# Banded attention feeding a two-layer MLP in split float32: slices of d_ff taken two at a time

## The chip, the cores and the metric

The kernel runs on one core of one Trainium2 chip. The metric is the device time of one execution in microseconds (us). The core has five engines that work side by side: TensorE (PE, matmuls; its weight loads are listed as PEld), VectorE (DVE), ScalarE (ACT), GpSimd (POOL) and SyncE (SP, which issues nearly all DMAs). Each engine works through its own queue in the order in which the built program lists its instructions.

## The reference

Attention over 4 batches, 8 heads, 768 positions and head dimension 64, with a distance bias and a mask (8 global keys and the 96 last ones), then an MLP over the 3072 tokens. Cut to what matters:

```
scores = q @ k.T / sqrt(D) - slope[h] * dist;  scores = where(keep, scores, -1e9)
a = softmax(scores);  x = a @ v                        # (3072, 512)
h = x @ w_in                                           # (3072, 2048), the first layer
g = h * clip(h + 3, 0, 6) / 6                          # the gate
out = g @ w_out                                        # (3072, 512), the second layer
```

The MLP's weights and activations are float32. The kernel gets float32 accuracy from the faster rounded format fp32r by splitting each operand into a high and a low part (`w1h` and `w1l`, `xh` and `xl`, `gh` and `gl`) and adding three products.

## The kernel before, in words

The tokens are cut into eight blocks of 384 (`blocks`, numbered 0 to 7). Each block takes the 16 slices of d_ff (`f`, 128 wide) in turn. For one slice of one block:

- `first(f, x)` (line 167) issues 12 matmuls of 384 columns into one of two PSUM banks, the tile `hp`.
- `gate` (178, 179) turns `hp` into `g`: ACT adds 3 and clips below, DVE clips above and multiplies. There is one buffer for `g`, so the next gate begins after the last reader of this one.
- `high` (185 on POOL, 187 on ACT while weights are being decoded) makes `gh`, and `rest` (192, DVE) makes `gl`.
- `second(f, acc, gh, gl)` (line 199) issues 9 matmuls of 512 columns that add the slice to three accumulators.

Below, F*n* is the first layer of slice *n* and S*n* its second one. `halves` writes them in the order F0, F1, S0, F2, S1, F3, S2 and so on: each second layer stands one first layer behind its own.

The weights arrive as raw 64-bit words. `decode` (lines 395 to 428) makes 32 chunks of 512 columns from them: chunk 2*f* is the first-layer weight of slice *f*, chunk 2*f*+1 the second-layer one. A chunk costs five DVE instructions (409, 410, 418, 422, and 415, which writes the low part `w1l` or `w2l`) and three on ACT (375, 387, and 426, which writes the high part `w1h` or `w2h`). The methods `work` and `decoded_to` slip decode steps in between the layers as the code is written. The order of PE, SP and POOL is then fixed as written (`in_order`); DVE and ACT are put in an order by the scheduler while the program is built. What stands in a queue is not moved at run time.

Attention work is handed out in numbered units that run at the `yield`s of the layer loops: `scores` (842, PE, with DVE 853 and ACT 857 behind it), `split` (813 on POOL, 816 and 819 on DVE), `normalize` (877, POOL), `spread` (902 on DVE, then a DMA to `there`), `fetch` (a DMA back into `weights`) and `values` (929, PE).

The stages are: attention for the first nine head pairs with three slices of block 0 (to about 64 us); then the rest of block 0 and half of block 1, mixed by the string `ORDER`, while the weights are decoded (to about 157 us); then the rest of block 1 with attention for block 2 ("one", to about 198 us); then blocks 2 to 7 ("layers"), each with the attention of the block after it.

Of the kernel before, what the change touches and what calls it, by code (L numbers as in the profile page):

```python
# [25 lines left out]
NF = DF // P  # L26
# [33 lines left out]
class Kernel:  # L60
# [45 lines left out]
    def common(self, xs, banks):  # L106
        self.xp = self.pool("xp", xs)
        self.w1h, self.w1l, self.w2h, self.w2l = [], [], [], []
        self.gp = self.pool("gp", 3)
        self.gp1 = self.pool("gp1", 1)  # L110
        self.ps_h = self.pool("ps_h", banks, PSUM)

# [174 lines left out]
    def load(self, n, values):  # L287

        if n < len(self.blocks) * NPAIR:
            end = KW + (TB if n < EARLY else QW)  # L290
            for columns in (slice(KW + QW, LOAD),) if values else (slice(0, KW), slice(KW, end)) if n == 0 else (slice(0, end),):
                self.nc.sync.dma_start(out=self.place(n)[:, columns], in_=self.pairs[n, :, columns])
# [155 lines left out]
    def halves(self, steps, pool=False):  # L448


        for block, f, x, acc in steps:
# [11 lines left out]
                yield  # L463
            self.last = (block, f, acc, gh, gl)

    def end(self, steps):

        x, acc = steps[0][2:]
        late = []
        for k, (_, f, _, _) in enumerate(steps):  # L470
            g = self.gate(self.first(f, x), f == NF - 1)
            gh = self.high(g, True)
            late.append((f, acc, gh, self.rest(g, gh)))
            if k == 0:
                self.finish()
            elif k == 1:
                self.second(*late[0], (0, 1))
        self.second(*late[0], (2,))
        self.second(*late[1], (0, 1))
        self.second(*late[2], (0, 1))  # L480
        self.second(*late[1], (2,))
        self.second(*late[2], (2,))
# [11 lines left out]
    def banded(self, flag):  # L494

        self.banded_setup()
        start = len(self.nc.cur_bb.bb.instructions)
        self.common(2, 2)
        self.ps_s = self.pool("ps_s", 1, PSUM)
        self.ps_t = self.pool("ps_t", 1, PSUM)  # L500
        self.ps_x = self.pool("ps_x", 1, PSUM)
        self.turn, self.stage = {}, "attention"
        self.wake()
        self.raw, self.z, self.e, self.given, self.decoded = {}, {}, {}, [0.0, 0.0], 0
        self.last, self.op = None, None
        self.weights()
        with ExitStack() as early, ExitStack() as words:
            x0 = self.x_tiles(self.pool("x0", 1, ctx=early, side="right"))
            xs = [x0, self.x_tiles(), self.x_tiles()]
            self.decoding(words, 3, 2, side="right")  # L510
            self.decoding_steps = self.decode()

            self.decoded_all = words.close
            self.fetch(0)
            self.given[1] = LEAD
            self.allowed = 4 * NF + 3
            acc = []
            with ExitStack() as ctx:
                self.room += self.rooms(self.pool("more", 1, ctx=ctx), MORE - ROOMS, ROOMS)
                self.load(2, False)  # L520
                self.fetch(1)
                for n in range(ROOMS):
                    self.load(n, True)
                self.plain_distances(ctx)
                self.attending(ctx, 0, 9, 5)
                pairs = [Pair(self, n, xs[n // NPAIR], True) for n in range(EARLY)]
                todo = self.halves([(0, f, xs[0], acc) for f in range(FIRST)])

                def half():
                    if self.stage == "both":  # L530
                        next(todo, None)

                for n in range(-2, EARLY + 1):
                    if n + 2 < NPAIR:
                        self.distances(n + 2)
                    if n + 2 == EARLY:
                        self.stage = "both"
                        acc.extend(self.acc_tiles())
                    if n + 2 < EARLY:
                        weigh = []  # L540
                        for t in range(NT):
                            weigh.append(pairs[n + 2].scores(t))
                            if n == 0 and t < NT - 1:
                                self.spin(2)
                        if n < 0:
                            self.spin(5)
                        self.load_next(n + 2, False)
                        self.work(1.440, 0)
                    for t in range(NT):
                        if n + 2 < EARLY:  # L550
                            weigh[t]()
                            self.work(0, 0.64)
                            if t == NT - 1 and n == -2:
                                self.load(2, True)
                        if 0 <= n < EARLY:
                            pairs[n].turn(t)
                            if n == 0 and t < NT - 1:
                                self.spin(3)
                            self.work(0.396, 0)
                        if n + 1 in (0, 1):  # L560
                            pairs[n + 1].sum_up(t)
                            pairs[n + 1].normalize(t)
                        if t == 0:
                            if 2 <= n + 1 < EARLY:
                                pairs[n + 1].sum_up()
                            half()
                        if t == 1:
                            if n > 0:
                                pairs[n - 1].values()
                                self.work(1.350, 0.47)  # L570
                            if 2 <= n + 1 < EARLY:
                                for u in range(NT):
                                    pairs[n + 1].normalize(u)
                        if t == 2:
                            half()
                for _ in todo:
                    pass
            self.weights()
            self.allowed = 4 * (2 * NF + 1)
            acc1 = [pool.tile([P, BANK], F32, name=name) for pool, name in ((self.ps_s, "sp"), (self.ps_t, "tp"), (self.ps_x, "xp"))]  # L580
            self.given[1] = max(self.given)
            next_f, todo = [FIRST, 0], []
            for block in map(int, ORDER):
                todo.append((block, next_f[block], xs[block], (acc, acc1)[block]))
                next_f[block] += 1
            for _ in self.halves(todo):
                pass
            self.decoded_to(2 * NF - 1)
        self.attending(self.ctx, 2, 3, 2, side="right")
        self.bp = self.pool("bp", 3, side="right")  # L590
        self.there = self.pool("there", 2, bass.MemoryType.DRAM)
        self.op = self.pool("op", 3, side="right")
        self.stage = "one"
        units, pairs = self.rest_of_third(xs[2], NF - next_f[1])
        for k, _ in enumerate(self.halves([(1, f, xs[1], acc1) for f in range(next_f[1], NF)], True)):
            for unit in units[k]:
                unit()
        self.finish()
        pairs[-2].values("s")
        self.stage = "layers"  # L600
        x, ahead = xs[2], pairs[-1]
        for i in range(2, len(self.blocks)):
            units, x_next = [], None
            if i + 1 < len(self.blocks):
                x_next = self.x_tiles()
                units, ahead = self.attention(i + 1, x_next, ahead)
            else:
                units = [[]] * 4 + [[lambda: self.doubt(flag)]]
            acc = self.acc_tiles()
            steps = [(i, f, x, acc) for f in range(NF)]  # L610
            for k, _ in enumerate(self.halves(steps if x_next else steps[:-3], True)):
                for unit in units[k] if k < len(units) else ():
                    unit()
            if not x_next:
                self.end(steps[-3:])
            x = x_next
        self.in_order(start)
        return acc
# [390 lines left out]
```

## Time and profile before

| | |
|---|---|
| Median of three timed runs | 663.02 us (662.13 to 663.42) |
| Span of the profiled execution | 660.9 us, 11414 instructions |
| What lies between that span and the median | 2.1 us |
| PE busy | 649.6 us, 98% |
| DVE, ACT, POOL busy | 65%, 44%, 31% |
| Granted TensorE clock, mean | 0.998 |

The profiled execution has no time of its own beside its span, so a forecast for the span is carried to the median by adding those 2.1 us. Matmuls overlap in the pipeline, and the profile models their ends; "busy" on PE therefore says only that one was under way. A timeline row gives a start, a duration, the engine, the line and the operands. In the chain of work that ended last, each row is a start, a length, and what filled it.

### The profile page before, as it was taken

What the parts mean: (1) busy time and instruction counts of PE and PEld (TensorE: products, weight loads), DVE (VectorE), ACT (ScalarE), POOL (GpSimd) and SP (SyncE); (2) the same over time, 40 slices, a digit from 0 to 9 for tenths busy, and PEclk for the clock granted to TensorE, in tenths of its full rate; (3) what the DMA queues carried; (4) which work ended last, traced back from release to release, by engine and by line L of the source; (5) the groups of instructions that cost most, each with busy time, mean ns of one, the idle gap of its engine ahead of it and who ended that gap; (6) DMA issues with size and microseconds to landing.
All of it is one profiled execution on the core that took longest, in us unless ns stands there. A gap on an engine that the chain in (4) does not pass through costs nothing.

```text
span 660.9 us, 11414 instructions
## 1 busy us (share of the span) xinstructions
PE 649.6 (98%) x3933; PEld 581.9 (88%) x3933; DVE 427.6 (65%) x1147; ACT 288.1 (44%) x752; POOL 202.2 (31%) x377
## 2 busy tenths in 40 slices
PE   9989999999999999999999999999999999999997
PEld 7768899998989999999989999899998999989995
DVE  6888999998856876367654777367663777422222
ACT  6896877776434343344314333143422443121111
POOL 5663000002533433034331553134340444312110
PEclk9999999999999999999999999999999999999999
DMA  8676445432582566536553557615654265510001
GB/s 284 178 233 215 132 157 159 132 124 89 158 224 95 156 175 172 143 100 162 153 153 96 135 137 185 180 51 143 165 138 128 95 160 131 133 49 1 1 1 53
DMA packets 67316, 88.86 MB, mean 134 GB/s; under 512 B 10288, under 2 KB 52016, under 8 KB 67248
## 3 DMA queue, kind: packets, MB, share of 16 engines
q1 hardware_dynamic: 66960, 87.77, 46.5%
q8 instruction: 33, 0.54, 0.3%
q14 instruction: 35, 0.29, 0.1%
q10 hardware_dynamic: 288, 0.26, 0.1%
HBM read 65.08 MB, written 22.94 MB: 133 GB/s over the span
## 4 chain that ended last, share of the span: by engine, by line
PE 86%; DVE 9%; ACT 2%; issue 2%; POOL 0%; POOLq 0%; DVEq 0%; ACTq 0%
PE hp L167 37%; PE acc L199 33%; PE xp L929 3%; PE sp L842 2%; PE tp L929 2%; PE tp L842 2%; PE sp L199 1%; ACT n L857 1%; DVE wz L422 1%; PE tp L199 1%; DVE wz L418 1%; PE xp L199 1%; DVE wz L410 1%; DVE g L179 1%; DVE gl L192 1%
## 5 line engine op out<-in xcount | busy, mean ns | idle before, releaser
L178 ACT ACTIVATE g<-hp,small 128x384 f32<-128x384 f32 x127 | 73.7, 580 | 253.3 <-PE hp L167 227.0
L167 PE MATMUL hp<-xh,w1h 128*128 128x384 f32 x512 | 174.1, 340 | 0.4 <-ACT w1h L426 0.4
L167 PE MATMUL hp<-xh,w1l 128*128 128x384 f32 x512 | 173.0, 338 | 0.5 <-DVE w1l L415 0.5
L167 PE MATMUL hp<-xl,w1h 128*128 128x384 f32 x512 | 171.9, 336 | 0.0
L185 POOL TENSOR_SCALAR gh<-g 128x384 fp32r<-128x384 f32 x104 | 55.6, 535 | 311.2 <-DVE g L179 279.7
L199 PE MATMUL acc<-w2h,gl 128*128 128x512 f32 x336 | 133.2, 396 | 0.2 <-DVE gl L192 0.2
L199 PE MATMUL acc<-w2l,gh 128*128 128x512 f32 x336 | 132.4, 394 | 0.0
L199 PE MATMUL acc<-w2h,gh 128*128 128x512 f32 x336 | 131.9, 393 | 0.0
L179 DVE SCALAR_TENSOR_TENSOR g<-g,hp 128x384 f32<-128x384 f32 x128 | 69.8, 545 | 69.7 <-ACT g L178 69.1
L877 POOL TENSOR_SCALAR n<-n,sums 128x232 f32<-128x232 f32 (+1 forms) x186 | 99.4, 549 | 32.2 <-DVE sums L868 17.6
L192 DVE TENSOR_TENSOR gl<-g,gh 128x384 fp32r<-128x384 f32 x128 | 78.4, 613 | 47.5 <-POOL gh L185 47.5
L857 ACT ACTIVATE n<-n,least 128x232 f32<-128x232 f32 (+1 forms) x192 | 89.0, 465 | 41.6 <-DVE least L853 40.3
L167 PEld LDWEIGHTS hp<-xh,w1h 128*128 128x128 f32 x512 | 96.3, 188 | 6.4 <-issue 1.7
L167 PEld LDWEIGHTS hp<-xl,w1h 128*128 128x128 f32 x512 | 96.2, 188 | 3.8
L167 PEld LDWEIGHTS hp<-xh,w1l 128*128 128x128 f32 x512 | 96.0, 188 | 1.0 <-DVE w1l L415 0.8
L199 PEld LDWEIGHTS acc<-w2h,gl 128*128 128x128 f32 x336 | 63.0, 187 | 15.1 <-DVE gl L192 1.6
L199 PEld LDWEIGHTS acc<-w2h,gh 128*128 128x128 f32 x336 | 63.3, 188 | 10.5 <-POOL gh L185 0.3
L199 PEld LDWEIGHTS acc<-w2l,gh 128*128 128x128 f32 x336 | 63.2, 188 | 10.3
L902 DVE STREAM_TRANSPOSE blocks<-n 128x256 f32<-128x256 f32 x127 | 48.8, 422 | 27.0 <-POOL n L877 26.8
L813 POOL TENSOR_SCALAR kx<-load 64x504 fp32r<-64x504 f32 (+1 forms) x46 | 35.3, 767 | 100.3 <-PE hp L167 96.2
L853 DVE CUSTOM_DVE_ANT_0 n<-sp,d 128x232 f32<-128x232 f32 (+1 forms) x70 | 23.7, 376 | 36.7 <-PE sp L842 36.5
L857 ACT ACTIVATION_READ_ACCUMULATOR n<-n,least 128x1 f32 x192 | 36.1, 188 | 0.0
(118 smaller groups left out, 746.4 us busy)
## 6 DMA issues: line engine op xcount, KB each, us to landing
wst<-w SPq DMA_DIRECT2D x32, 512.0 KB, 3.5
there<-blocks SPq DMA_DIRECT2D x58, 256.0 KB, 2.6
load<-pairs SPq DMA_DIRECT2D x23, 636.0 KB, 5.1
load<-pairs SPq DMA_DIRECT2D x32, 384.0 KB, 4.3
weights<-there SPq DMA_DIRECT2D x48, 192.0 KB, 3.8
weights<-there SPq DMA_DIRECT2D x44, 160.0 KB, 3.2
out<-o SPq DMA_DIRECT2D x23, 256.0 KB, 2.2
load<-pairs SPq DMA_DIRECT2D x8, 444.0 KB, 4.4
```

What stands on the lines that cost most here:

```text
L167: self.nc.tensor.matmul(hp, lhsT=self.w1(w, f)[:, kt, :], rhs=a[:, kt, :], start=(n == 0), stop=(n == 3 * NKT - 1))
L178: nc.scalar.activation(out=g, in_=hp, func=AF.Relu, bias=self.three, scale=1.0)
L179: nc.vector.scalar_tensor_tensor(out=g, in0=g, scalar=6.0, in1=hp, op0=ALU.min, op1=ALU.mult)
L185: self.nc.gpsimd.tensor_scalar(out=gh, in0=g, scalar1=1.0, scalar2=0.0, op0=ALU.mult, op1=ALU.add)
L192: self.nc.vector.tensor_tensor(out=gl, in0=g, in1=gh.bitcast(F32), op=ALU.subtract)
L199: self.nc.tensor.matmul(acc[tt], lhsT=a[:, tk], rhs=self.w2(w, f), start=(f == 0 and j == 0), stop=(f == NF - 1 and j == 2))
L813: nc.gpsimd.tensor_scalar(out=part["kx"][own, c], in0=k[own, c], scalar1=1.0, scalar2=0.0, op0=ALU.mult, op1=ALU.add)
L842: nc.tensor.matmul(sp[j][:, lo:W], lhsT=q[:, t], rhs=part["kx"][:, c], start=(m == 0), stop=(m == 1))
L857: nc.scalar.activation(out=e[:, j, lo:W], in_=e[:, j, lo:W], func=AF.Exp, bias=self.least[:, i:i + 1], scale=-1.0, accum_out=self.sums[:, ...
L877: nc.gpsimd.tensor_scalar(out=e[:, j, lo:W], in0=e[:, j, lo:W], scalar1=over, scalar2=0.0, op0=ALU.mult, op1=ALU.add)
L902: nc.vector.transpose(out=blocks[:, :, s].rearrange("p b j q -> p j b q"), in_=e[:, :, c:c + P].rearrange("p j (b q) -> p j b q", b=4))
L929: nc.tensor.matmul(xps[j * D:(j + 1) * D, t * P:(t + 1) * P], lhsT=vt[0:K, t, j * D:(j + 1) * D], rhs=self.part(t, j, c, K), start=(c == 0 ...
```

## The change

`halves` is replaced by `twos` wherever it stood after the first nine pairs: in the mixed turns of blocks 0 and 1, in the rest of block 1, and in blocks 2 to 7. `twos` writes two first layers, each followed by its gate and both halves of `g`, then the two second layers of the pair before. To hold two pairs of results, the pool of `gh` and `gl` grows from three buffers each to four, and the pool of output tiles `o` shrinks from three to two. In `twos` the step that makes `gh` and `gl` stands right behind the gate in the code. There are four `yield`s for two slices, as before, but two of them follow both first layers and two follow both second ones.

```diff
-        self.gp = self.pool("gp", 3)
+        self.gp = self.pool("gp", 4)
...
+    def twos(self, steps, pool=False):
+        for i in range(0, len(steps), 2):
+            after = []
+            for block, f, x, acc in steps[i:i + 2]:
+                self.decoded_to(2 * f)
+                g = self.gate(self.first(f, x))
+                gh = self.high(g, pool)
+                after.append((block, f, acc, gh, self.rest(g, gh)))
+                self.work(2.1, 0.94)
+                if i == 0 and len(self.pending) == 1:
+                    self.last = self.pending[0]
+                    self.finish()
+                    self.pending = []
+            yield
+            yield
+            for self.last in self.pending:
+                self.finish()
+            self.pending = after
+            yield
+            yield
...
-            for _ in self.halves(todo):
+            self.pending = [self.last]
+            for _ in self.twos(todo):
...
-        self.op = self.pool("op", 3, side="right")
+        self.op = self.pool("op", 2, side="right")
...
-        for k, _ in enumerate(self.halves([(1, f, xs[1], acc1) for f in range(next_f[1], NF)], True)):
+        for k, _ in enumerate(self.twos([(1, f, xs[1], acc1) for f in range(next_f[1], NF)], True)):
...
-            for k, _ in enumerate(self.halves(steps if x_next else steps[:-3], True)):
+            for k, _ in enumerate(self.twos(steps if x_next else steps[:-3], True)):
```

Three places in the built program show it. The first is PE's queue in the mixed turns, where slice 7 of block 0 ends. Before (`hp_1383` is the result of slice 7, `hp_1430` that of slice 8; `gh_1364` and `gl_1366` belong to slice 3 of block 1):

```order
L167 MATMUL hp_1383<-xh_147,w1l0_141 128x384
L199 MATMUL sp_1027<-w2h0_142,gh_1364 128x512
L199 MATMUL sp_1027<-w2l0_143,gh_1364 128x512
L199 MATMUL sp_1027<-w2h0_142,gl_1366 128x512
L199 MATMUL tp_1028<-w2h0_142,gh_1364 128x512
L199 MATMUL tp_1028<-w2l0_143,gh_1364 128x512
L199 MATMUL tp_1028<-w2h0_142,gl_1366 128x512
L199 MATMUL xp_1029<-w2h0_142,gh_1364 128x512
L199 MATMUL xp_1029<-w2l0_143,gh_1364 128x512
L199 MATMUL xp_1029<-w2h0_142,gl_1366 128x512
L167 MATMUL hp_1430<-xh_147,w1h1_1023 128x384
```

Now, with `hp_1368` for slice 7 and `hp_1405` for slice 8:

```order
L167 MATMUL hp_1368<-xl_148,w1h0_140 128x384
L167 MATMUL hp_1368<-xh_147,w1l0_141 128x384
L167 MATMUL hp_1405<-xh_147,w1h1_1023 128x384
L167 MATMUL hp_1405<-xl_148,w1h1_1023 128x384
L167 MATMUL hp_1405<-xh_147,w1l1_1024 128x384
```

The nine matmuls of a second layer have gone from between the two first layers.

The second place is DVE's queue at the same point, where the low part of slice 8's first-layer weights is written (`w1l1_1024`; its raw words are in `wz_1359` before and `wz_1363` now). Before:

```order
L409 TENSOR_SCALAR wz_1400<-wz_1400 128x512
L192 TENSOR_TENSOR gl_1366<-g_1354,gh_1364 128x384
L410 TENSOR_SCALAR wz_1400<-wz_1400 128x512
L415 TENSOR_TENSOR w1l1_1024<-wz_1359,w1h1_1023 128x4x128
L418 SCALAR_TENSOR_TENSOR wz_1400<-wst_1336,wz_1400 128x512
L179 SCALAR_TENSOR_TENSOR g_1396<-g_1396,hp_1383 128x384
```

Now:

```order
L409 TENSOR_SCALAR wz_1395<-wz_1395 128x512
L179 SCALAR_TENSOR_TENSOR g_1381<-g_1381,hp_1368 128x384
L410 TENSOR_SCALAR wz_1395<-wz_1395 128x512
L415 TENSOR_TENSOR w1l1_1024<-wz_1363,w1h1_1023 128x4x128
L418 SCALAR_TENSOR_TENSOR wz_1395<-wst_1356,wz_1395 128x512
L192 TENSOR_TENSOR gl_1386<-g_1381,gh_1384 128x384
```

The gate of slice 7 stood behind slice 8's weights and now stands ahead of them. In the pair of slices 12 and 13 the queue reads the same way, with a line 418 between the gate and the weights.

The third place is POOL's queue in a block of the last stage, around the last head pair's `normalize`. Before:

```order
L185 TENSOR_SCALAR gh_3883<-g_3880 128x384
L813 TENSOR_SCALAR kx_3908<-load1_73 64x504
L813 TENSOR_SCALAR kx_3913<-load1_73 64x504
L877 TENSOR_SCALAR n_3837<-n_3837,sums_3835 128x128 x2
L877 TENSOR_SCALAR n_3858<-n_3858,sums_3835 128x232 x2
L185 TENSOR_SCALAR gh_3938<-g_3935 128x384
L877 TENSOR_SCALAR n_3886<-n_3886,sums_3835 128x232 x2
```

Now (line 813 has become 839, and 877 has become 903):

```order
L185 TENSOR_SCALAR gh_3894<-g_3891 128x384
L839 TENSOR_SCALAR kx_3910<-load1_73 64x504
L839 TENSOR_SCALAR kx_3915<-load1_73 64x504
L903 TENSOR_SCALAR n_3839<-n_3839,sums_3837 128x128 x2
L903 TENSOR_SCALAR n_3849<-n_3849,sums_3837 128x232 x2
L903 TENSOR_SCALAR n_3899<-n_3899,sums_3837 128x232 x2
L185 TENSOR_SCALAR gh_3982<-g_3979 128x384
```

The `gh` that stood inside the six `normalize` instructions now stands outside them.

More of the change, by code (lines that the diff above doesn't have):

```diff
@@ L474, in end @@
             if k == 0:
-                self.finish()
+                for self.last in self.pending:
+                    self.finish()
             elif k == 1:
@@ L591, in banded @@
         self.there = self.pool("there", 2, bass.MemoryType.DRAM)
-        self.op = self.pool("op", 3, side="right")
+        self.op = self.pool("op", 2, side="right")
         self.stage = "one"
         units, pairs = self.rest_of_third(xs[2], NF - next_f[1])
-        for k, _ in enumerate(self.halves([(1, f, xs[1], acc1) for f in range(next_f[1], NF)], True)):
+        for k, _ in enumerate(self.twos([(1, f, xs[1], acc1) for f in range(next_f[1], NF)], True)):
             for unit in units[k]:
                 unit()
-        self.finish()
+        for self.last in self.pending:
+            self.finish()
+        self.pending = []
         pairs[-2].values("s")
```

## The prediction

> **What bounds the kernel now.** The page comes first: who is busy, and whose work makes up the chain that ended last.
>
> ```profile
> PE 649.6 (98%) x3933; PEld 581.9 (88%) x3933; DVE 427.6 (65%) x1147; ACT 288.1 (44%) x752; POOL 202.2 (31%) x377
> PEclk9999999999999999999999999999999999999999
> PE 86%; DVE 9%; ACT 2%; issue 2%; POOL 0%; POOLq 0%; DVEq 0%; ACTq 0%
> ```
>
> TensorE is under way for 649.6 of 660.9 us at the full clock, so time is won or lost only by its idle time or by the spacing of its matmuls. The chain still has 9% of DVE in it. Two stretches, from the busy times by window (in order: us, PE, PEld, DVE, ACT, POOL, clock, DMA share, GB/s), and the DVE instructions of the decoding stage, grouped over 67 to 150 us, tell where:
>
> ```profile
> 80.00:100.00 20.00, 20.00 (x101) 18.04 (x100) 19.40 (x39) 15.26 (x29) 0.00 (x0) 1.00 0.49 152
> 200.00:590.00 390.00, 390.00 (x2374) 354.54 (x2373) 239.98 (x651) 138.10 (x392) 138.02 (x238) 1.00 0.49 133
> L179 DVE SCALAR_TENSOR_TENSOR g<-g,hp 128x384 f32<-128x384 f32 x20 | 11.0, 551 | 3.1 <-ACT g L178 3.0
> L415 DVE TENSOR_TENSOR w1l<-wz,w1h 128x512 fp32r<-128x512 f32 x12 | 8.2, 686 | 0.0
> ```
>
> While weights are decoded DVE is busy 19.40 of 20 us beside a PE busy 20.00, and what DVE does wait for there is the gate, 3.1 us in all. DVE and PE are level, and a weight chunk is ready just in time. From 200 to 590 us DVE has 150 us to spare and PE never stops. So the change is costed in two parts: the decoding stage by when the weights come, the rest by what the matmuls' order does to their spacing.
>
> **Decoding: what a first layer waits for.** The waits of PE before, and the place of the largest:
>
> ```profile
> PE hp L167 <- DVE w1l L415: 0.5, 1, 0.5
> PE hp L167 <- ACT w1h L426: 0.4, 1, 0.4
> PE acc L199 <- DVE gl L192: 0.2, 1, 0.2
> 149.15 0.39 PE L199 MATMUL xp<-w2h,gl 128*128 128x512 f32 x1
> 149.97 0.45 PE L167 MATMUL hp<-xh,w1h 128*128 128x384 f32 x1 [0.44 <-ACT w1h L426]
> 151.06 0.44 PE L167 MATMUL hp<-xh,w1l 128*128 128x384 f32 x1 [0.47 <-DVE w1l L415]
> ```
>
> F15 of block 0 should start .23 after 149.15, at 149.38, and reach its third matmul (the first to use `w1l`) .35 later, at 149.73; it does so at 151.06. That is 1.3 us, 1.4 with a slow restart.
>
> In the new order the two first layers of a pair stand next to each other. Where both belong to block 0, the second needs a new chunk 2.1 us earlier, for the S between them is gone: pairs (7, 8) and (12, 13). The DVE rows for both as they run now:
>
> ```profile
> 100.13 0.42 DVE L410 TENSOR_SCALAR wz<-wz 128x512 int32<-128x512 int32 x1
> 100.47 0.69 DVE L415 TENSOR_TENSOR w1l<-wz,w1h 128x512 fp32r<-128x512 f32 x1
> 101.07 0.69 DVE L418 SCALAR_TENSOR_TENSOR wz<-wst,wz 128x512 int32<-128x512 int32 x1
> 101.90 0.56 DVE L179 SCALAR_TENSOR_TENSOR g<-g,hp 128x384 f32<-128x384 f32 x1
> 102.37 0.69 DVE L422 CUSTOM_DVE_ANT_0 wz<-wz,we 128x1024 uint16<-128x1024 uint16 x1
> 134.68 0.40 PE L199 MATMUL sp<-w2h,gh 128*128 128x512 f32 x1
> 135.49 0.55 DVE L179 SCALAR_TENSOR_TENSOR g<-g,hp 128x384 f32<-128x384 f32 x1 [0.31 <-ACT g L178]
> 136.30 0.69 DVE L415 TENSOR_TENSOR w1l<-wz,w1h 128x512 fp32r<-128x512 f32 x1
> 137.10 0.38 PE L167 MATMUL hp<-xh,w1l 128*128 128x384 f32 x1
> ```
>
> The last four rows are slices 12 and 13. F12 hands over at 134.68, its gate starts on DVE .81 later (with ACT's half in between), `w1l` of slice 13 is done at 136.99, and F13's third matmul runs at 137.10: S6, 2.08 us long, just covers it. Take S6 away and F13 waits. From the hand-over of F12: .81 to the gate, .47 from gate to the next instruction (101.90 to 102.37), .60 for line 418 (100.47 to 101.07 for an instruction as long), .69 for `w1l`: 2.57. Wanted at .35, so 2.2 us, with the slow restart 2.3. For slices 7 and 8, line 410 (.34, from 100.13 to 100.47) stands where 418 does: 2.31 against .35, 2.0, with the restart 2.1. These two do not depend on how far DVE has come: the gate of the pair's first slice is ahead of the second's weights in DVE's queue, and that gate cannot start before its F is over.
>
> Two smaller ones follow from arriving early. From the chain of work, with DVE's rows beside it:
>
> ```profile
> 69.17 2.12 PE hp L167 x12
> 73.68 2.10 PE hp L167 x12
> 75.78 0.47 PE acc L199 x2
> 78.15 2.12 PE hp L167 x12
> 73.06 0.69 DVE L415 TENSOR_TENSOR w1l<-wz,w1h 128x512 fp32r<-128x512 f32 x1
> 79.87 0.69 DVE L415 TENSOR_TENSOR w1l<-wz,w1h 128x512 fp32r<-128x512 f32 x1
> ```
>
> A first layer takes 2.12 us in block 0 and 2.10 in block 1, a second one 2.08. In the new order F3, F1, F4 follow from 69.17; F4 begins at 73.39 and needs its `w1l` (done at 73.75) at 73.6: .2 us. Then S0, S3, and F5 begins at 79.9, wants `w1l` at 80.1 and gets it at 80.56: .5 us. New waits: .2 + .5 + 2.1 + 2.3 = 5.1 us.
>
> What goes: S0 and S3 after 71.29 and 75.78 took 2.39 and 2.37 instead of 2.08 (a second layer that comes close behind its own gate, the wait for `gl` in the list; now a whole pair lies between them), .6; and the 1.4 at F15, which then has its weights, since three gate instructions (3 x .47) leave the queue ahead of `w1l` of slice 15 and PE comes 3 us later. Net for the stage: 5.1 - 2.0 = +3.1 us. Bounds: if DVE gains the whole 3.1 us that it waits for gates, F4 and F5 wait for nothing and +2.4 is left; if every other chunk also slips by one gate (.47) on the way, about +4.
>
> **The rest: spacing.** The end of the chain holds one first layer that follows a second layer of six matmuls instead of nine:
>
> ```profile
> 645.34 2.10 PE hp L167 x12
> 647.44 1.39 PE acc L199 x6
> 648.83 2.08 PE hp L167 x12
> ```
>
> Both have 12 equal matmuls; the usual one is .02 longer. A first layer right behind another does not occur in the trace. Its bounds are nothing gained (2.10) and the same 2.08; I take 2.08, the nearest row in which the usual switch is missing. About 60 second members of pairs x .02 = 1.2 us; I take back .2, since at a switch the first matmul starts a few ns sooner. The `scores` are gathered too, eight matmuls at a time instead of four; fewer switches there, at most .3 us by the same .02. Gain: 1.2 us, bounds 0 and 2.
>
> **What stays hidden.** The other links of the gate's chain, and the stores, from the page:
>
> ```profile
> L178 ACT ACTIVATE g<-hp,small 128x384 f32<-128x384 f32 x127 | 73.7, 580 | 253.3 <-PE hp L167 227.0
> L185 POOL TENSOR_SCALAR gh<-g 128x384 fp32r<-128x384 f32 x104 | 55.6, 535 | 311.2 <-DVE g L179 279.7
> L192 DVE TENSOR_TENSOR gl<-g,gh 128x384 fp32r<-128x384 f32 x128 | 78.4, 613 | 47.5 <-POOL gh L185 47.5
> out<-o SPq DMA_DIRECT2D x23, 256.0 KB, 2.2
> ```
>
> The gates come in bursts, but a slice's `gh` and `gl` are wanted one pair later, 8.4 us, where it was one F and one S. The single `g` buffer makes the second gate wait for the first one's `gl`; the chain ACT, DVE, POOL, DVE is .58 + .55 + .53 + .61 = 2.3 us, with hand-overs some 2.7, twice in 8.4. The `hp` bank is needed again 6.3 us after its F, as before. With two output buffers the third store of a block waits on ACT for the first DMA to land, 2.2 us; S0's first tile is 4.2 us of F away and its third 5.6; SP's queue behind it holds the next block's `there` writes, 8 us off. If that cover failed, each block boundary would cost what is left of 2.2. `values` is the one place with little room. The last pair's scores, its fetch, and its values:
>
> ```profile
> 326.69 0.61 PE L842 MATMUL sp<-kx,q 128*128 128x232 f32 x4
> 339.69 1.74 SPq L911 DMA_DIRECT2D weights<-there  x4
> 346.06 1.21 PE L929 MATMUL xp<-weights,load 128*64 128x128 f32 x18
> DMA to landing us min/median/max: 2.5/3.5/5.1
> ```
>
> The last scores end at about 327.2, the fetch is issued by 341.4 and has landed by 344.9: 17.7 us. The last pair's own values come second, 1.3 us after 346.06: 20.2 us after the scores. In the new order two SS and two FF lie between instead of five S and four F, 2.1 us less: 18.1. It still fits by .4, and POOL no longer has a `gh` between the `normalize`s. I cost it at nothing.
>
> **Sum.** +3.1 - 1.2 = +1.9 us. Span 660.9 + 1.9 = 662.8; with the 2.1 us between span and median, 663.02 + 1.9 = 664.9 us. About .2% (1.3 us) is what a measurement of this kernel can tell from no change, so this lies just beyond it, on the slower side.
>
> **Rivals.**
> *The switch is worth more.* If a switch between the two shapes costs not .02 but s us, the gain is 60 s. At s = .045 it eats most of the 3.1 and the time is about 663.4, no change; from s = .073 it wins 4.4 us and the kernel is faster, 661.7 or less. For it: FF and SS have no row of their own. Against it: 2.10 against 2.08 leaves no room, unless a second layer behind another were shorter than 2.08 as well.
> *The values come late.* Should the gates now bunched ahead of DVE's and POOL's attention work lengthen the fetch chain beyond 18.1 us, PE waits at the last pair of each of five blocks: with 1 us each, +5, 669.9. The point is .4 us above today's 17.7. For it: `kx` and two `gh` stand ahead of the first `normalize`. Against it: as many instructions as before, and DVE with a third of its time free.
> *The clock drops in the waits.* If TensorE fell to half clock for one layer after each of the two 2 us waits, 2 x 2.1 = 4.2 more: 669.1. Before, it waited for up to 1.4 us at one place and the clock row stayed at 9:
>
> ```profile
> PE xp L929 <- issue: 1.4, 1, 1.4
> ```
>
> [...]
>
> **Chances.** Forecast (the two waits at 7/8 and 12/13, little regained) .56, 664.4 to 666.0. Switch worth more, to no change, .24; on to faster, .08. Values late .10. Clock .02. So slower .68, same .24, faster .08. Range for 8 in 10: from 662.9 (the upper half of "no change" in, its lower part and faster out) to 668.0 (values late by up to .6 us a block).
>
> **What would show it.** Right: PE waits of about 2 us for `w1l` in F8 and F13 of block 0, near 100 and 136 us, none at F15; PE without idle time after 200 us; second members of pairs at 2.08 in the chain. Wrong: no wait there; waits of PE on `weights` or on `acc`; a clock row below 9; first layers at 2.10 throughout (then 666), or pairs much shorter than 8.36 us.

## The result, and the profile after

| | before | after |
|---|---|---|
| Median, range, runs | 662.95 us (662.13 to 663.42), 4 | 672.28 us (667.62 to 672.66), 4 |
| Ratio after to before | | 1.0125 (95% interval 1.0095 to 1.0156) |
| Span of the profiled execution | 660.9 us | 670.6 us |

The kernel became 9.3 us slower, where 1.9 us had been forecast; 672.3 lies outside the range of 662.9 to 668.0. From the page of the changed kernel, the lines on busy time, clock and the chain:

```profile
PE 650.7 (97%) x3933; PEld 583.9 (87%) x3933; DVE 424.3 (63%) x1147; ACT 286.4 (43%) x752; POOL 189.0 (28%) x377
PEclk9999999989998999999999999999999999999999
PE 87%; DVE 6%; ACT 2%; issue 2%; DMA 2%; POOL 1%; SPq 0%; POOLq 0%; ACTq 0%; DVEq 0%
```

Two slices of the clock row have fallen to 8, and DMA has entered the chain. The busy times by stage (in order: us, PE, PEld, DVE, ACT, POOL, clock, DMA share, GB/s) tell where the time went. Before, the mixed turns, the rest of block 1, block 2, and block 3:

```profile
64.73:155.00 90.27, 89.30 (x443) 79.56 (x442) 84.75 (x170) 68.12 (x121) 1.73 (x2) 1.00 0.43 134
155.00:198.98 43.98, 43.98 (x275) 38.96 (x273) 31.13 (x92) 19.99 (x59) 16.25 (x33) 1.00 0.64 182
198.98:275.32 76.34, 76.34 (x473) 69.55 (x472) 49.31 (x133) 27.12 (x77) 26.58 (x48) 1.00 0.56 152
275.32:352.70 77.38, 77.38 (x465) 70.28 (x464) 46.20 (x127) 27.55 (x79) 27.71 (x48) 1.00 0.49 137
```

The same four stages after:

```profile
64.79:160.35 95.56, 90.52 (x444) 80.98 (x442) 87.44 (x174) 68.34 (x122) 1.43 (x2) 0.98 0.39 127
160.35:206.51 46.16, 44.25 (x274) 38.99 (x272) 29.45 (x87) 19.28 (x57) 16.56 (x32) 1.00 0.61 172
206.51:284.99 78.48, 76.16 (x464) 69.29 (x463) 49.27 (x133) 27.07 (x78) 25.50 (x48) 0.98 0.56 152
284.99:361.90 76.91, 76.91 (x466) 70.11 (x464) 45.68 (x128) 27.09 (x79) 24.70 (x48) 1.00 0.49 134
```

The mixed turns take 5.3 us more, the rest of block 1 2.2 more. Block 2 takes 2.1 more although nine matmuls of a second layer (2.08 us) have left it for the end of block 7, so it lost 4.2. From block 3 on, a block takes .39 to .47 us less. The waits of PE after, those of half a microsecond and more that were not there before or have grown:

```profile
PE hp L167 <- ACT w1h L426: 2.4, 2, 1.2
PE hp L167 <- ACT xh L153: 1.8, 1, 1.8
PE hp L167 <- DVE g L179: 1.6, 1, 1.6
...
PE acc L955 <- DMA weights<-there: 1.2, 1, 1.2
PE hp L167 <- DVE w1l L415: 1.1, 2, 0.7
...
PE acc L868 <- DVE kx L845: 0.6, 2, 0.4
```

The rows for `w1h` and `w1l` are slices 8 and 13 of block 0, the places that the prediction named. The other four it did not expect. And the waits are not all: behind two of them TensorE ran slowly. The timeline around slice 13 (start, duration, engine, line; in brackets the idle time before the row, and what ended it):

```profile
136.96 0.44 PE L167 MATMUL hp<-xh,w1h 128*128 128x384 f32 x1 [1.18 <-ACT w1h L426]
137.24 0.33 PE L167 MATMUL hp<-xl,w1h 128*128 128x384 f32 x1
138.24 0.44 PE L167 MATMUL hp<-xh,w1l 128*128 128x384 f32 x1 [0.68 <-DVE w1l L415]
...
139.79 0.53 PE L167 MATMUL hp<-xh,w1h 128*128 128x384 f32 x1
140.12 0.53 PE L167 MATMUL hp<-xl,w1h 128*128 128x384 f32 x1
...
141.18 0.63 PE L199 MATMUL acc<-w2l,gh 128*128 128x512 f32 x1
141.61 0.63 PE L199 MATMUL acc<-w2h,gl 128*128 128x512 f32 x1
...
143.04 0.39 PE L199 MATMUL acc<-w2h,gh 128*128 128x512 f32 x1
```

From start to start, matmuls of 384 columns take 320 ns there instead of 175, and those of 512 columns 427 instead of 230: half clock, from about 139.3 to 142.7 us. The same happens from 211.0 to 214.4. A ledger of the profiled executions, in us, from the start-to-start times of the layers, slow restarts included (behind a wait the second matmul starts .28 us after the first, 136.96 to 137.24 above, instead of .175):

| Stage | Difference | Made of |
|---|---|---|
| mixed turns | +5.3 | slice 4 +1.9; slice 8 +2.1; slice 13 +2.4; half clock behind it +1.6; gone: slice 15 -1.4, S0 and S3 -.6; spacing and small waits -.6 |
| rest of block 1 | +2.2 | last `values` +1.3; scores +1.0 |
| block 2 | +4.2 | `xh` and `xl` +2.4; half clock behind it +1.7; scores +.65; spacing -.5 |
| blocks 3 to 7 | -2.2 | spacing |

### The profile page after: what moved, and what is told of

It is laid out like the page before. It is cut to its first block, busy times and chain, and to the rows that moved or that the text cites. A ratio compares the mean times of both kernels' runs of the same rounds, so it can differ in the third digit from the quotient of the medians.

```text
span 670.6 us, 11409 instructions
## 1 busy us (share of the span) xinstructions
PE 650.7 (97%) x3933; PEld 583.9 (87%) x3933; DVE 424.3 (63%) x1147; ACT 286.4 (43%) x752; POOL 189.0 (28%) x377
## 4 chain that ended last, share of the span: by engine, by line
PE 87%; DVE 6%; ACT 2%; issue 2%; DMA 2%; POOL 1%; SPq 0%; POOLq 0%; ACTq 0%; DVEq 0%
PE hp L167 37%; PE acc L199 34%; PE xp L955 3%; PE sp L868 2%; PE tp L955 2%; PE tp L868 2%; PE sp L199 1%; PE tp L199 1%; PE xp L199 1%; ACT n L883 1%; DVE n L879 1%; DMA out<-o 1%; DMA wst<-w 1%; POOL n L903 1%; PE xp L362 1%
## 5 line engine op out<-in xcount | busy, mean ns | idle before, releaser
L185 POOL TENSOR_SCALAR gh<-g 128x384 fp32r<-128x384 f32 x104 | 53.4, 513 | 293.8 <-DVE g L179 255.3
L903 POOL TENSOR_SCALAR n<-n,sums 128x232 f32<-128x232 f32 (+1 forms) x186 | 94.4, 525 | 53.7 <-DVE sums L894 44.5
L192 DVE TENSOR_TENSOR gl<-g,gh 128x384 fp32r<-128x384 f32 x128 | 75.6, 591 | 48.9 <-POOL gh L185 48.8
L839 POOL TENSOR_SCALAR kx<-load 64x504 fp32r<-64x504 f32 (+1 forms) x46 | 29.1, 633 | 119.2 <-PE hp L167 99.4
L845 DVE TENSOR_TENSOR kx<-load,kx 64x504 fp32r<-64x504 f32 (+1 forms) x46 | 32.4, 705 | 4.7 <-POOL kx L839 3.3
```

The source lines that it names most:

```text
L185: self.nc.gpsimd.tensor_scalar(out=gh, in0=g, scalar1=1.0, scalar2=0.0, op0=ALU.mult, op1=ALU.add)
L192: self.nc.vector.tensor_tensor(out=gl, in0=g, in1=gh.bitcast(F32), op=ALU.subtract)
L839: nc.gpsimd.tensor_scalar(out=part["kx"][own, c], in0=k[own, c], scalar1=1.0, scalar2=0.0, op0=ALU.mult, op1=ALU.add)
L845: nc.vector.tensor_tensor(out=part["kx"][other, c], in0=k[own, c], in1=part["kx"][own, c].bitcast(F32), op=ALU.subtract)
L903: nc.gpsimd.tensor_scalar(out=e[:, j, lo:W], in0=e[:, j, lo:W], scalar1=over, scalar2=0.0, op0=ALU.mult, op1=ALU.add)
```

## The experiments

Each time below is a median. Kernels of one batch share the runs of the kernel before, 662.7 to 662.9 us. In the experiments' rows the line numbers are a few higher (168 or 170 for 167). "Three o" stands for one edit that nearly all of them carry: three output buffers fit into the memory if `gl` gets three buffers of its own and only `gh` keeps four.

```
+        self.glp = self.pool("glp", 3)
-        gl = self.gp.tile([P, TB], F32R, name="gl")
+        gl = self.glp.tile([P, TB], F32R, name="gl")
-        self.op = self.pool("op", 2, side="right")
+        self.op = self.pool("op", 3, side="right")
```

### The third output buffer: two runs

First the changed kernel with "three o" alone.

> The changed kernel with three output buffers again (to make room, the low parts gl of the gate get three buffers and the high parts gh keep four). Theory: at the end of block 1 the third output tile waits on ACT for the first tile's store to land (5.7 us in the trace after), ACT's copy into xh stands behind it, and block 2's second layer-one matmul group waits 1.8 + .4 us for it; with the wait of 1.2 us just before it, this also halves the clock for some 3 us (11 matmuls x .145 = 1.6 us). All of that goes: 672.3 - 3.8 = 668.5, the copy xh no longer behind out<-o, full clock between 210 and 214. Rival A (the store is only the wait that is seen, and the values' own fetch chain is late): no more than .5 us is won, 671.8. Rival B (the half clock at 210 has another cause, an electrical or periodic one): the waits go, the slow matmuls stay, 670.1.

It took 668.56 us (665.88 to 672.23), ratio to before 1.0103 (1.0058 to 1.0148), 3.7 less than the changed kernel. What had held block 2 back is read from the chain of work of the changed kernel (start, length, what filled it):

```profile
202.71 0.61 ACT o L56
...
203.34 5.68 DMA out<-o
...
209.12 0.07 ACT o L56
...
209.62 0.48 ACT xh L153
```

The third output tile waits for the first one's store to land, 5.68 us, and `xh` stands behind it in ACT's queue. With three buffers, in ACT's timeline, the third tile follows the second at once:

```profile
201.10 0.60 ACT L56 ACTIVATE o<-tp 128x512 f32<-128x512 f32 x1
201.78 0.60 ACT L56 ACTIVATE o<-xp 128x512 f32<-128x512 f32 x1
204.38 0.48 ACT L154 CAST xh<-acc 128x384 fp32r<-128x384 f32 x1 [2.00 <-PE acc L956]
```

Block 2 went from 78.48 to 74.78 us in the profile. Rival A falls. That the medians differ by the same 3.7 is in part luck: in the profile slice 4 also waits 1.0 us less, which this edit does not touch. The runs of this kernel lie 6 us apart, by their mean clock: at 1.0 and .999 the spans are 664.6 and 664.0, at .993 and .992 they are 668.8 and 670.4. So .7 to .8% of missing clock goes with 4 to 6 us, and it comes and goes with the same program.

Then the pools alone, in the kernel before:

```
-        self.gp = self.pool("gp", 3)
+        self.gp = self.pool("gp", 4)
-        self.op = self.pool("op", 3, side="right")
+        self.op = self.pool("op", 2, side="right")
```

> The kernel before, order of layers untouched, with the changed pools alone: four gh and gl, two output buffers. Theory: the store of block 1 takes 5.3 us to land in the trace before as well, so the same wait appears at the start of block 2 by the buffer alone: xh late by about 2 us, 663.0 + 2 = 665; 666.6 if the clock falls as well. The other block ends stay without a wait, since nobody waits on ACT there. Rival (the prediction's): hidden, as before to .2%, 663.0.

665.16 us (664.39 to 665.40), ratio 1.0038 (1.0024 to 1.0053): +2.3, with every layer in its old place. The chain shows the same links, with 3.78 us for the store:

```profile
197.13 3.78 DMA out<-o
...
201.51 0.48 ACT xh L153
```

Blocks 3 to 7 are as before, to .02 us. The buffer costs at this one block end, by itself, and nothing at the others.

### Pairs in one stage only: blocks 2 to 7, and the mixed turns

`twos` for blocks 2 to 7, `halves` elsewhere, three o:

```
-            for _ in self.twos(todo):
+            for _ in self.halves(todo):
...
-        for k, _ in enumerate(self.twos([(1, f, xs[1], acc1) for f in range(next_f[1], NF)], True)):
+        for k, _ in enumerate(self.halves([(1, f, xs[1], acc1) for f in range(next_f[1], NF)], True)):
...
```

> Pairs in blocks 2 to 7 alone; the mixed turns and the rest of block 1 run as before, with three output buffers and three gl. Theory: only the spacing is left, which the trace after shows as .39 to .47 us a block (blocks 3 to 7); six blocks make 2.5 us: 663.0 - 2.5 = 460.5 + 200 = 660.5. The prediction's term: 1.2 us, 661.8. Rival (three gl make DVE and then PE wait): some .4 us for each of 44 pairs shows on DVE, and if it reached PE, 663 or more.

(The "460.5 + 200" in it is a slip for 660.5.) 660.84 us (660.13 to 661.56), ratio .9967 (.9955 to .9980): faster than before by about 2 us. The busy times of blocks 2 and 3:

```profile
198.84:274.22 75.38, 74.24 (x464) 67.79 (x463) 49.38 (x133) 26.43 (x77) 25.48 (x48) 1.00 0.57 156
274.22:351.13 76.91, 76.91 (x466) 70.13 (x464) 45.72 (x128) 27.16 (x79) 24.59 (x48) 1.00 0.48 134
```

Block 3 has its 76.91 again, so the gain belongs to the order of the layers and not to the other stages. Block 2 has 1.1 us of idle time. Nothing is pending at its start, so eight scores and four units come without a layer between them; that costs .65 us in scores. Another 1.0 us is lost at its second `values` in this profile. The same block in the same order loses 0 to .4 us there in the other five profiles, so this second part is not shown to come from the order.

Then `twos` in the mixed turns alone, `halves` in the rest of block 1 and in blocks 2 to 7, three o:

```
-        for k, _ in enumerate(self.twos([(1, f, xs[1], acc1) for f in range(next_f[1], NF)], True)):
+        (self.last,), self.pending = self.pending, []
+        for k, _ in enumerate(self.halves([(1, f, xs[1], acc1) for f in range(next_f[1], NF)], True)):
...
-            for k, _ in enumerate(self.twos(steps if x_next else steps[:-3], True)):
+            for k, _ in enumerate(self.halves(steps if x_next else steps[:-3], True)):
...
```

> Pairs in the mixed turns of blocks 0 and 1 alone; the rest of block 1 and blocks 2 to 7 run as before, with three output buffers. Theory: the stage costs what it costs in the trace after, 95.55 - 90.27 = +5.3 us: a wait of 1.8 for an hp bank at the third first layer in a row, 1.9 and 2.2 at slices 8 and 13, half clock for 1.6 us behind the last, less 2.0 for what vanishes: 668.2. The prediction's sum for this stage: +3.1, 666.1. If the half clock needs the later waits at block 2, it is missing here: 666.7.

667.41 us (666.10 to 668.42), ratio 1.0070 (1.0052 to 1.0088). The stage takes 95.1 us in the profile, and the half clock is there without any of the later waits: the extra condition in the expectation falls, the theory's 668.2 is .8 too high. Of four runs three had a mean clock of .994 to .997 and 667.2 to 668.4 us, and one 1.0 and 666.1.

### Is it the wait that lowers the clock?

The kernel of the last run, with seven matmuls of no use ahead of the first layers of slices 8 and 13, into the bank that the layer overwrites:

```
+        for _ in range(fill):
+            self.nc.tensor.matmul(hp, lhsT=self.w1(self.w1h, f - 1)[:, 0, :], rhs=x[0][:, 0, :], start=True, stop=True)
...
-                g = self.gate(self.first(f, x))
+                g = self.gate(self.first(f, x, 7 if block == 0 and f in (8, 13) else 0))
```

> Pairs in the mixed turns alone, as in the run with 667.4 us, plus seven matmuls of no use (384 columns, into the bank that the next first layer overwrites) ahead of the first layers of slices 8 and 13, where TensorE waits 1.3 us for w1h. They fill 7 x .175 = 1.2 us of the wait and lengthen nothing. Theory (the half clock comes from too little matmul work in a stretch of some microseconds): idle time ahead of slice 13 falls from 1.9 to .7 us, no matmul takes 320 ns any more, every run shows a mean clock of .998 or more (without the filling .994, .996, .997 and 1.0), and the time is that of the one run at full clock, 666.1. Rival A (the clock falls by itself, by time or by load): slow matmuls in most runs still, 667.4. Rival B (the seven stand in the way): the first layers start later, up to .2 us each, 667.8.

665.92 us (665.72 to 667.19), mean clock 1.0 in all four runs. By window, around slice 13, without the filling and with it:

```profile
133.00:139.00 6.00, 4.16 (x20) 3.52 (x20) 4.98 (x12) 3.49 (x7) 0.00 (x0) 0.94 0.53 151
139.00:143.00 4.00, 4.00 (x14) 3.36 (x14) 3.86 (x9) 3.42 (x7) 0.00 (x0) 0.67 0.52 158
```

```profile
133.00:139.00 6.00, 5.33 (x29) 4.74 (x28) 5.01 (x11) 3.19 (x7) 0.00 (x0) 1.00 0.37 107
139.00:143.00 4.00, 4.00 (x20) 3.43 (x19) 3.97 (x10) 3.69 (x7) 0.00 (x0) 1.00 0.42 153
```

PE is busy 5.33 us of the first six instead of 4.16, and the clock of the next four is 1.00 instead of .67. The useful work starts no earlier: only the clock is won, 1.5 us by the medians. Rivals A and B fall.

The same filling in a version with "three o" and `halves` in the rest of block 1 (its unfilled form comes below, 665.37 us) tests whether the parts add up.

> The changed kernel with three output buffers and the rest of block 1 slice by slice (665.37 us; 664.1 to 666.2, mean clock .996 to 1.0), plus the seven matmuls of no use ahead of the first layers of slices 8 and 13. Pairs are left in the mixed turns and in blocks 2 to 7. Theory (the parts add up): the mixed turns cost 665.9 - 662.9 = +3.0 us at full clock, blocks 2 to 7 give 660.8 - 662.9 = -2.1: 663.8, clock .998 or more in every run, and the spread between runs shrinks to about 1 us. Rival (the runs of the version without filling differ for another reason than the clock behind these two waits): 665.4 with the same spread of 2 us.

663.84 us (663.33 to 665.22, 11 runs), ratio 1.0016 (1.0007 to 1.0025), every mean clock .998 or more. Forecast: 663.8; ten of the eleven runs lie within .8 us.

### The pairs of slices of one block

The changed kernel with three o, and a pending second layer written between the two first ones where both slices belong to block 0:

```
-                if i == 0 and len(self.pending) == 1:
-                    self.last = self.pending[0]
+                if self.pending and (i == 0 and len(self.pending) == 1 or [t[0] for t in steps[i:i + 2]] == [0, 0]):
+                    self.last = self.pending.pop(0)
                     self.finish()
-                    self.pending = []
```

> The changed kernel with three output buffers (668.56 us; 665.9 to 672.2), in which the two pairs of slices of block 0 alone (7 with 8, 12 with 13) are written as before: a second layer stands between the two first ones. Everything else goes in pairs. Theory: the waits for w1h and w1l at these slices (1.34 + .57 and 1.34 + .83 = 4.1 us) go, and the low clock behind them; at most 1 us of it comes back at a later slice. 663.5 to 664.5, clock .997 or more in nearly all runs, the mixed stage 93.0 - 4 = 89 to 90 us (90.3 before). Rival (DVE is behind in any order, the waits only move to the next slice of block 0): 667 to 668.

The mixed stage takes 90.3 us, near the forecast 89 to 90, and its waits are down to these two:

```profile
PE hp L168 <- DVE g L180: 0.7, 1, 0.7
PE hp L168 <- DVE w1l L416: 0.7, 2, 0.3
```

But the time is 665.93 us (663.55 to 669.47, 10 runs), above the 663.5 to 664.5. Of the 4.5 us that the two pairs had lost, 1.6 came back in later slices, where at most 1 had been allowed. The stage gave 2.7 us by the two profiles (93.0 to 90.3) and the medians 2.6, so the low clock did not go: the mean clocks are still .994 to 1.0. PE now arrived 2.9 us earlier at the last `values` of block 1, waited 2.5 us there for their fetch instead of 1.3, and ran slowly behind that wait:

```profile
198.00:203.00 5.00, 2.48 (x24) 1.79 (x22) 0.00 (x0) 1.32 (x3) 0.00 (x0) 0.91 1.02 223
203.00:206.00 3.00, 3.00 (x12) 2.91 (x11) 0.56 (x1) 0.48 (x1) 0.00 (x0) 0.59 1.04 388
```

### The first pair

Three first layers stood in a row at the start of the mixed turns, F3, F1, F4, since the pending second layer was written inside the first pair. In the kernel with filled waits that second layer now stands behind the pair:

```
-                if i == 0 and len(self.pending) == 1:
-                    self.last = self.pending[0]
-                    self.finish()
-                    self.pending = []
```

> Pairs in the mixed turns alone with the filled waits (665.92 us, clock 1.0 in all runs); the pending second layer is now written behind the first pair instead of between its two first layers, so the order is F0 F3 S2 F1 F4 instead of F0 S2 F3 F1 F4. Theory: slice 4 waited up to 1.74 us for its hp bank because three first layers in a row use two banks; that goes, 665.9 - 1.7 = 664.2. Rival (slice 3 comes 2.1 us earlier and waits for its own weights, or slice 4 then waits for w1l): .4 to 1.7 of it comes back, 664.6 to 665.9.

665.79 us (665.07 to 666.05) against 665.92: no difference that can be told. The waits of PE up to 85 us, without the edit and with it:

```profile
PE hp L170 <- DVE g L182: 1.6, 1, 1.6
```

```profile
PE hp L170 <- DVE w1l L418: 0.6, 2, 0.3
```

The wait for the bank is gone, as the theory said, and in its place slices 4 and 5 wait for `w1l`, as the rival said: their pairs take 4.88 and 4.81 us where an undisturbed one takes 4.21, together 1.3 us, against 1.9 at slice 4 before. The .6 us between is not lost later: from the start of these turns to the next `scores` the profile takes .6 us less (97.6 instead of 98.2). But it began the turns .4 us later, before anything that the edit touches, so a gain of this size is lost in the spread of the runs.

### The rest of block 1, and block 2

The changed kernel with three o, and `halves` in the stage "one":

```
-        for k, _ in enumerate(self.twos([(1, f, xs[1], acc1) for f in range(next_f[1], NF)], True)):
+        (self.last,), self.pending = self.pending, []
+        for k, _ in enumerate(self.halves([(1, f, xs[1], acc1) for f in range(next_f[1], NF)], True)):
...
```

> The changed kernel with three output buffers, with the rest of block 1 (the stage one) written slice by slice as before, pairs elsewhere. Theory: the stage takes 44.0 us as before instead of 46.2: the 1.2 to 1.5 us for the last values' fetch and the 1.0 us in bunched scores go. 668.6 - 2.2 = 666.4, less where the clock fell behind that wait. Rival (the wait only moves into block 2, whose first scores are bunched as well): 668.

665.37 us (664.06 to 666.20), ratio 1.0036 (1.0022 to 1.0050); the stage is back to its time before:

```profile
158.53:202.49 43.96, 43.93 (x275) 39.07 (x273) 28.74 (x87) 19.54 (x58) 16.05 (x32) 1.00 0.63 180
```

2.2 us in the stage, 3.2 by the medians; the rest goes with the clock (.996 to 1.0 here, .992 to 1.0 there). This does not make the whole 2.2 a cost of the pairs: a wait of .9 to 1.3 us for the same fetch shows in three other profiles below in which this stage is written as before. The scores' 1.0 us do not.

Next, pairs in blocks 2 to 7 with one `yield` behind each layer:

```
                 after.append((block, f, acc, gh, self.rest(g, gh)))
                 self.work(2.1, 0.94)
+                yield
-            yield
-            yield
             for self.last in self.pending:
                 self.finish()
+                yield
             self.pending = after
-            yield
-            yield
```

> Pairs in blocks 2 to 7 alone (660.84 us), but with one yield behind every first and every second layer instead of two behind a pair: four scores stand behind each layer again, the order F F S S stays. Theory: block 2, where this version lost .65 us in scores and 1.0 us in values because eight scores and four units came at once, takes 73.7 us instead of 75.4, and the gain in spacing (.39 to .47 us a block) stays: 660.8 - 1.6 = 659.2. Rival (the gain in spacing comes from second layers that stand directly behind each other, and scores between them take it away where there are scores): blocks 3 to 6 go back by some .2 us each, 660.0 or more.

660.71 us (660.33 to 661.83), ratio .9967 (.9953 to .9981), no better than 660.84. Theory and rival were both right, in their own blocks:

```profile
199.72:273.58 73.86, 73.86 (x464) 67.68 (x462) 48.85 (x132) 26.53 (x76) 26.81 (x48) 1.00 0.55 154
273.58:350.70 77.12, 77.12 (x466) 70.26 (x465) 46.71 (x129) 27.99 (x80) 25.51 (x48) 1.00 0.52 143
```

Block 2 gains the 1.5 us, .6 of it in the scores and 1.0 in the wait at `values` that comes and goes; block 3 gives back .2 of its .47, for its layers no longer stand in unbroken pairs. So: spread units in block 2 only, whole pairs from block 3 on (`single` chooses the `yield`s of the last edit or those of the change):

```
-            for k, _ in enumerate(self.twos(steps if x_next else steps[:-3], True)):
+            for k, _ in enumerate(self.twos(steps if x_next else steps[:-3], True, i == 2)):
```

> Pairs in blocks 2 to 7 alone (660.84 us), with one yield behind each layer in block 2 only, where eight scores at once cost .65 us, and two behind a pair in blocks 3 to 7, where the gain in spacing was .39 to .47 us a block and with spread scores only .2 to .35. Theory: 75.4 to 73.9 in block 2, the rest as in that run: 660.8 - 1.2 = 659.6. Rival (what block 2 loses is the fetch of the values before it, which varies from run to run): 660.5.

660.34 us (659.95 to 662.19), ratio .9957 (.9943 to .9970). It is the fastest version tried, and faster than before and after. Block 2 takes 73.9 us as the theory had it, yet the time lies near the rival's 660.5 and not at 659.6. That it beats the plain version by more than the spread is not shown. Its profiled execution, the slowest of its five, still waits here, in the rest of block 1, which it runs as the kernel before does:

```profile
PE acc L959 <- DMA weights<-there: 1.3, 1, 1.3
```

Last, all repairs at once, with pairs in the mixed turns as well: to the last edit comes `twos(todo)` with the first pair whole and, in `twos`,

```
+                if [t[0] for t in steps[i:i + 2]] == [0, 0] and len(after) == 1:
+                    self.last = self.pending.pop(0)
+                    self.finish()
```

> Pairs everywhere but at three places: the two pairs of block 0 are split by a second layer (as in the run with 665.93 us), the rest of block 1 goes slice by slice (665.37 us), and block 2 has one yield behind each layer (73.86 us there). The first pair of the mixed turns is no longer broken by the pending second layer, so three first layers never stand in a row. Three output buffers, three gl. Theory (all that the change cost were these places and the buffer): stage by stage from the traces 89.4 + 43.95 + 73.86 + 76.91 + 77.81 + 76.91 + 77.81 + 71.17 = 587.8 against 591.3 before: 662.9 - 3.5 = 659.4. Rival (the mixed turns are bound by DVE, and what is won there comes back as later waits): mixed stage 90.3 as before, 660.3.

660.81 us (660.51 to 662.07), ratio .9966 (.9954 to .9978). The mixed stage takes 90.7 us, not 89.4, with DVE busy for 86.2 of them; four waits of about .3 us for `w1l` are left. The window of the stage, and then the row of its waits:

```profile
64.38:155.04 90.66, 89.38 (x444) 79.37 (x442) 86.20 (x174) 68.83 (x122) 1.94 (x2) 1.00 0.43 134
```

```profile
PE hp L168 <- DVE w1l L416: 1.3, 4, 0.3
```

In this stage pairs win nothing over the 90.3 of before, and the medians agree (660.81 against 660.34 without them): the rival was right.

## Why the prediction was wrong, step by step

In the profile the change lost 9.7 us where 1.9 had been forecast. Two terms of the sum were off: the mixed turns at full clock cost 3.7 instead of 3.1, and spacing from block 2 on gave 2.7 instead of 1.2. Four costs were not in the sum: the low clock (3.3), the output buffer (2.4), the rest of block 1 (2.2) and the scores of block 2 (.65).

**The two large waits: right in place and size.** Slice 8 is delayed by 2.1 us and slice 13 by 2.4, slow restarts included, forecast 2.1 and 2.3; at slice 15 there is none. DVE's chain ran as priced. The prediction looked at `w1l` alone, though, and PE's longer wait is the one for `w1h`: ACT's half of slice 12's gate (at 135.81) stands ahead of slice 13's `w1h` (136.29) in ACT's queue.

**"The `hp` bank is needed again 6.3 us after its F, as before": wrong in the first turn.** It holds once two second layers stand between pairs. In the first turn they do not, F4 is the third first layer in a row, and it was delayed by 1.9 us until the gate of F3 had left the bank, where .2 had been priced. F3's matmuls are over at about 71.5; its gate runs on ACT at 73.09, behind `w1h` of slice 4, and on DVE at 74.45, behind `w1l`. How late it comes varies: in the seven profiles with this first turn the idle time there is .6 to 1.6 us. When the first pair is whole, slices 4 and 5 wait .4 and .5 us for `w1l`, restarts apart, where .2 and .5 were forecast. So the waits on weights were read well, and the bank was not looked at in this turn.

**"With two output buffers ... 2.2 us", costed at nothing: wrong.** 2.2 was the median over 23 stores. At the one place where ACT's next instruction is wanted at once, the end of block 1, the trace of before had already shown another number. Its DMA issues from 196.5 to 204 us (the last column is the time to landing):

```profile
out<-o SPq DMA_DIRECT2D x3, 256.0 KB, 5.3
```

The buffer alone cost 2.3 us by the medians.

**The rest of block 1 had no term.** The change was costed "in two parts", the decoding stage and the spacing behind it; the stage between them bunches its scores, and that is 1.0 us, with up to 1.3 more for a fetch that varies. The start of block 2, where again nothing is pending, was missed in the same way: .65 us in scores.

**The clock, at .02: wrong, and the largest single miss.** No run showed that waits of 2.0 and 2.3 us leave the clock as it is: the longest in the trace of before is 1.4 us. What the changed kernel's trace shows is half clock behind 1.74 and 1.94 us of idle time in 3.41 us, as the last section has it. That rival asked for "half clock for one layer after each of the two 2 us waits" and 4.2 us. It came behind one of those two and behind the waits at block 2, 1.6 and 1.7 us in the profile, 3.3 together. The run of the changed kernel at a mean clock of .999 took 667.6 us, the three at .993 to .996 took 672.1 to 672.7.

**The spacing: right in kind, too small in size.** Forecast 1.2 us, bounds 0 and 2; blocks 3 to 7 show .39 to .47 each, 2.2 in all, and block 2 some .5 more: 2.7, above the upper bound. The chain of the changed kernel:

```profile
566.25 4.17 PE hp L167 x24
570.42 0.44 PE sp L868 x4
570.87 4.12 PE acc L199 x18
```

Two second layers take 4.12 and not 2 x 2.08. The prediction's argument against this, that 2.10 against 2.08 "leaves no room, unless a second layer behind another were shorter than 2.08 as well", names what happened: over block 3 a matmul of a second layer takes 230.7 ns instead of 233.6, one of a first layer 175.4 instead of 176.7. So most of it came from the second layers, on which the forecast had no row. The gathered `scores`, from which up to .3 us was hoped, take .2 more a block (5.31 us instead of 5.12 in block 3).

**`values` in blocks 3 to 7: right.** They never wait in the profile after; the .4 us of room is thin, though, for the version with 660.81 us loses .8 us there in block 4, and that with 660.34 us .5.

## What to carry to other kernels

An order that is sound in the steady state must be walked through again at its first turn and at each seam between stages, buffer by buffer. A wait is priced with the duration at its own place, not with a median over the kernel. And where TensorE is the bound, two waits close together, 1.2 and .7 us here, can cost nearly as much again in clock (1.6 us); seven matmuls into a bank that is overwritten next kept it up.

## What the runs showed of the hardware that was not expected

The clock fell behind short gaps: 1.18 and .68 us of idle time within 3 us. It fell for about 3.4 us each time, to 320 and 427 ns a matmul, and only in some runs: the profile of the version with three output buffers has the same two waits at slice 13, 1.2 us for `w1h` and .7 for `w1l`, and a clock of 1.00 behind them.

The traces keep the moments at which the granted clock changes. In the changed kernel it is at half from 139.30 to 142.72 us and from 210.98 to 214.40, 3.41 us each. Here are the 3.41 us ahead of each of the two and the slow stretch itself (the clock is the third figure from the end):

```profile
135.89:139.30 3.41, 1.67 (x8) 1.36 (x9) 2.87 (x6) 2.68 (x6) 0.00 (x0) 1.00 0.36 117
139.30:142.72 3.42, 3.42 (x11) 3.05 (x10) 3.25 (x7) 2.94 (x6) 0.00 (x0) 0.50 0.52 144
207.57:210.98 3.41, 1.47 (x7) 0.89 (x6) 0.56 (x1) 0.97 (x2) 0.00 (x0) 1.00 0.37 138
210.98:214.40 3.42, 3.42 (x12) 3.42 (x12) 1.11 (x2) 0.58 (x1) 0.51 (x1) 0.50 0.55 150
```

Cut into stretches of this length, counted from the first change of the clock, the changed kernel's trace has three with 1.74, 1.94 and 2.78 us of idle time (the last one at the end of the kernel), each with half clock behind it. In the other 192 it is 1.41 us or less, and the clock behind them is 1.00. The version with three output buffers, cut in the same way, has these two at slice 13:

```profile
135.56:138.97 3.41, 2.04 (x10) 1.73 (x11) 3.21 (x7) 2.68 (x6) 0.00 (x0) 1.00 0.33 94
138.97:142.39 3.42, 3.42 (x18) 2.89 (x17) 3.28 (x7) 2.93 (x6) 0.00 (x0) 1.00 0.42 122
```

Here the stretch begins inside the first wait, and 1.37 us of idle time are left in it instead of 1.74. That the same wait counts in one run and not in the next for this reason is an estimate from these rows. Idle time is counted here from the modelled ends of the matmuls.

The fetch `weights<-there` ahead of block 2 made PE wait by 0 to 1.3 us in profiles whose stage is written in the same way as in the kernel before; its cause was not followed up.
